# Layer 2 of a squared-relu network by seven half-size products in place of eight, behind relative-bias attention

## Chip, cores and metric

One core of a Trainium2 chip (trn2). The metric is the device time of one execution in microseconds, of the slowest core (here the only one). Executions of one kernel differ by 0.2 to 1.3%. A part of the spread goes with the clock that TensorE was granted.

## The reference

Attention with a bias that depends on the distance of query and key (8 batches, 8 heads, 576 positions, 64 channels a head), whose output, as 4608 tokens of 512 channels, goes through two layers with a squared relu:

```python
scores = scale * q @ k.T + bias[bucket(|i - j|)]
x = softmax(scores) @ v                  # -> [4608, 512]
h = maximum(x @ w_in, 0.0)               # w_in  [512, 2048]
out = (h * h) @ w_out                    # w_out [2048, 512], float32 out
```

## The kernel before

The program is written as a list of operations with assumed durations. A small scheduler (`Plan`) places them in time, each engine taking the earliest ready operation, and the instructions are emitted in that order. The order of every engine is therefore fixed ahead; at run time an engine only waits for the results it needs. Changing any duration or constant reorders all engines.

The tokens go through the two layers in nine groups of 512 (`GT`). Layer 1 of a group is 16 blocks of four matmuls; each is followed by a relu on ScalarE and a square on VectorE into `g`. Layer 2 of the group before runs between those blocks:

```python
# layer 2 of group g-1, before
tiles = [(m, 0, 512) for m in range(4)]
if g == NG:
    tiles[-1:] = [(3, 0, 256), (3, 256, 256)]     # the very last tile in halves
for m, c0, cn in tiles:
    bank = Buf(r_g)                                # one of 3 PSUM banks
    for part in range(4):
        def f2(...):
            for nt in range(4 * part, 4 * part + 4):
                nc.tensor.matmul(g_ps[bank.slot][:, 0:cn], gs[gb.slot][:, nt, ts(m, 128)],
                                 w_out_sb[:, nt, c0 : c0 + cn], start=(nt == 0), stop=(nt == 15))
        ...
    # then one eviction PSUM -> y (ScalarE or VectorE, scaled) and a store
```

Attention of later batches runs in between as well. Its product with v uses one PSUM bank (`pv`) for both of its parts, so the second part waits until VectorE has taken the reciprocal and normalised the first (`x`). The PSUM tiles are two double banks for scores, one for `pv`, three for everything of the layers.

q and k are staged by whole batches (`NSTG` = 2), turned on TensorE for the first three batches (`DT_QK` = 3) and by transposing DMA after that.

The softmax here doesn't subtract the row's maximum and nothing guards it: scores larger than these inputs give would overflow.

## Time and profile before

| | before |
|---|---|
| time, median (all runs) | 388.05 us (387.28 to 388.28) |
| span in the profile | 385.6 us |
| TensorE, ScalarE, VectorE, GpSimd busy | 96%, 68%, 51%, 41% |
| layer 2: matmuls, spacing | 560 of 512 columns at 216 ns and 32 of 256 at 109 ns |
| TensorE idle from 40 us to the last group (369 us) | 0.2 us |

TensorE's busy share is modelled, and matmuls overlap in it (a 512-column one is listed with 380 ns but the next starts 216 ns later). So the spacing from start to start is what counts. The prediction below shows the lines and how to read them.

### The profile page before, as it was taken

How to read it: one execution, taken by the hardware profiler on the slowest of the kernel's cores; microseconds unless marked ns; L12 is line 12 of the kernel's file. 1: busy time of each engine (PE TensorE's matmuls, PEld its weight loads, DVE VectorE, ACT ScalarE, POOL GpSimd, SP SyncE). 2: the span in 40 equal slices, each digit the busy share in tenths (PEclk: the TensorE clock that was granted, in tenths of full speed). 3: DMA queues.
4: the chain of work that ended last, by engine and by line, in shares of the span. 5: the costliest groups of instructions: out<-in, count | busy, mean ns of one | idle time of the engine just before them, and what ended most of it. 6: DMA issues, size and time to landing. Idle time of an engine off the chain costs nothing.

```text
span 385.6 us, 8906 instructions
## 1 busy us (share of the span) xinstructions
PE 369.8 (96%) x3544; PEld 201.1 (52%) x3544; DVE 194.9 (51%) x494; ACT 263.9 (68%) x378; POOL 157.2 (41%) x286
## 2 busy tenths in 40 slices
PE   2879999999999999999999999999999999999996
PEld 2557455664545455554557855454544555444444
DVE  5889563965635555564526653555356452422200
ACT  2898985888856886787767876957478653634421
POOL 7984710679446544747454455535420000000000
PEclk9999999999999999999999999999999999999999
DMA  7999994499988999969989699889940122001012
GB/s 102 147 201 175 176 191 55 53 108 93 131 113 133 98 119 108 139 79 143 112 136 88 85 102 159 88 92 114 137 115 27 36 73 73 0 27 54 31 54 83
DMA packets 144202, 39.04 MB, mean 101 GB/s; under 512 B 130592, under 2 KB 139680, under 8 KB 144160
## 3 DMA queue, kind: packets, MB, share of 16 engines
q0 software_dynamic: 94432, 18.36, 60.8%
q1 hardware_dynamic: 49488, 19.98, 24.7%
q8 instruction: 28, 0.46, 0.5%
q10 hardware_dynamic: 240, 0.13, 0.2%
q14 instruction: 14, 0.11, 0.1%
HBM read 36.87 MB, written 9.44 MB: 120 GB/s over the span
## 4 chain that ended last, share of the span: by engine, by line
PE 90%; DVE 3%; DMA 3%; ACT 2%; issue 1%; SPq 1%; POOL 0%; DVEq 0%; ACTq 0%
PE f L914 33%; PE f L864 31%; PE pv L759 9%; PE st L622 8%; PE pv L752 3%; PE st L671 2%; PE st L646 2%; DMA kt<-ks 1%; DMA far_sb<-in_bias_table_dram 1%; PE f L577 1%; ACT pt L633 1%; DVE pt L714 1%; DVE qt L541 1%; PE f L326 1%; DVE x L781 0%
## 5 line engine op out<-in xcount | busy, mean ns | idle before, releaser
L633 ACT ACTIVATE pt<-st 128x1024 f16<-128x1024 f32 x128 | 126.5, 1023 | 35.1 <-PE st L622 35.0
L864 PE MATMUL f<-w_out_sb,g 128*128 128x512 f16 (+1 forms) x592 | 141.2, 374 | 0.0
L914 PE MATMUL f<-xt,w_in_sb 128*128 128x512 f16 (+1 forms) x640 | 140.1, 358 | 0.2 <-ACT xt L539 0.2
L935 ACT ACTIVATE rt<-f 128x512 f16<-128x512 f32 x144 | 85.5, 599 | 41.6 <-PE f L914 40.4
L945 DVE TENSOR_TENSOR g<-rt 128x512 f16<-128x512 f16 x144 | 60.6, 421 | 67.9 <-ACT rt L935 67.0
L914 PEld LDWEIGHTS <-w_in_sb 128*128 128x128 f16 x640 | 59.5, 98 | 61.5 <-issue 9.6
L864 PEld LDWEIGHTS <-g 128*128 128x128 f16 x592 | 54.3, 98 | 59.6 <-issue 8.1
L714 DVE TENSOR_TENSOR pt<-pt,tb_sb 128x512 f16<-128x512 f16 (+2 forms) x96 | 58.9, 624 | 35.8 <-ACT pt L633 35.7
L759 PE MATMUL pv<-va,pt 128*128 128x65 f16 x1280 | 54.6, 193 | 0.0
L759 PEld LDWEIGHTS <-pt 128*128 128x128 f16 x1280 | 50.2, 97 | 4.6 <-issue 0.3
L604 POOL COPY qz<-qt 64x64 f16<-64x64 f16 x55 | 16.3, 297 | 78.1 <-DMA qt<-qs 46.9
L255 POOL DMA_DIRECT2D qs<-in_q_dram x57 | 40.7, 731 | 4.9 <-PE f L914 3.4
L622 PE MATMUL st<-qt,kt 64*128 64x512 f16 x256 | 40.2, 386 | 2.6 <-ACT pt L633 1.2
L255 POOL DMA_DIRECT2D ks<-in_k_dram x57 | 40.8, 749 | 1.4 <-DMA ks<-in_k_dram 1.0
L752 PE MATMUL pv<-vm,pm 128*128 128x130 f16 x160 | 35.4, 221 | 0.3 <-DVE x L781 0.3
L884 ACT ACTIVATE y<-f 128x512 f32<-128x512 f32 (+1 forms) x25 | 14.5, 580 | 26.1 <-PE f L864 25.8
L781 DVE TENSOR_TENSOR x<-pv,r 128x384 f16<-128x384 f32 x64 | 31.3, 489 | 1.7
L604 POOL COPY kz<-kt 64x64 f16<-64x64 f16 x53 | 14.8, 278 | 41.4 <-DMA kt<-ks 36.1
L776 DVE RECIPROCAL r<-pv 128x6 f32<-128x6 f32 x64 | 12.0, 187 | 37.7 <-PE pv L759 37.7
L255 POOL DMA_DIRECT2D va<-in_v_dram x36 | 30.8, 877 | 0.3
L681 ACT ACTIVATE pm<-st 128x576 f16<-128x576 f32 x32 | 20.8, 651 | 3.7 <-PE st L671 3.6
L656 ACT ACTIVATE pt<-st 128x512 f16<-128x512 f32 x32 | 19.2, 599 | 5.2 <-PE st L646 5.1
(49 smaller groups left out, 164.5 us busy)
## 6 DMA issues: line engine op xcount, KB each, us to landing
out_dram<-y SPq DMA_DIRECT2D x35, 256.0 KB, 2.3
va<-in_v_dram POOLq DMA_DIRECT2D x28, 128.0 KB, 6.2
qs<-in_q_dram POOLq DMA_DIRECT2D x40, 64.0 KB, 3.1
ks<-in_k_dram POOLq DMA_DIRECT2D x40, 64.0 KB, 3.1
w_in_sb<-in_moe_w_in_dram POOLq DMA_DIRECT2D x4, 512.0 KB, 7.2
w_out_sb<-in_moe_w_out_dram POOLq DMA_DIRECT2D x4, 512.0 KB, 9.1
xt<-x SPq DMA_TRANSPOSE x48, 3.0
qs<-in_q_dram POOLq DMA_DIRECT2D x4, 144.0 KB, 5.0
```

What stands on the lines that cost most here:

```text
L255: lambda: io(eng.dma_start(out=out_(), in_=in_())),
L604: io(eng.tensor_copy(out=dst[qb.slot][rw, rw], in_=src[qb.slot][rw, 512:576]))
L622: nc.tensor.matmul(sets_ps[st.slot][:, e, :], kt[rw, ts(jt, 128)], qt[rw, 0:512], start=True, stop=True,)
L633: nc.scalar.activation(out=p5(pts[pb.slot])[:, jt, :, 0:512], in_=sets_ps[st.slot], func=EXPF, scale=SCALE)
L714: io(nc.vector.tensor_tensor(out=a, in0=a, in1=t, op=MULT))
L752: nc.tensor.matmul(ps[:, i, :, :], pm[:, c : c + 128], vm[:, hp, :, 0:65], start=True, stop=False)
L759: nc.tensor.matmul(ps[:, i, e, :], pt[:, (2 * jt + e) * S + c : (2 * jt + e) * S + c + 128], va[:, jt, 2 * hp + e, 0:65], start=False, sto ...
L781: nc.vector.tensor_tensor(out=xs[xb.slot][:, hp, qt0 : qt0 + nq, :].rearrange("p t (e d) -> p t e d", e=2), in0=ps[:, :, :, 0:64], in1=rs[ ...
L864: nc.tensor.matmul(g_ps[bank.slot][:, 0:cn], gs[gb.slot][:, nt, ts(m, 128)], w_out_sb[:, nt, c0 : c0 + cn], start=(nt == 0), stop=(nt == 15),)
L914: nc.tensor.matmul(g_ps[bank.slot][:, a:z], w_in_sb[:, kk, ts(nt, 128)], xt_sb[:, kk, c : c + z - a], start=(kk == 0), stop=(kk == 3),)
L935: io(nc.scalar.activation(out=rts[rb.slot], in_=g_ps[bank.slot], func=RELUF))
L945: nc.vector.tensor_tensor(out=gs[gb1.slot][:, nt, :], in0=rts[rb.slot], in1=rts[rb.slot], op=MULT)
```

## The change

Split the 512 tokens of a group and the 2048 inner and 512 output channels of layer 2 in two each. The ordinary product then needs eight products of quarter matrices; Strassen's scheme (in Winograd's form) needs seven, at the price of sums: four of weights (once), four of activations (each group) and additions when the products are evicted. VectorE had half its time free, TensorE none, so work is moved from the one to the other.

Activations are the quarters `a11 a12 / a21 a22`. With S1 = a21 - a22, S2 = a11 - S1, S3 = a21 - a11, S4 = a12 - S2 (signs folded into the weight sums T), the products are taken in the order 1, 2, 6, 5, 3, 7, 4, in the last group 1, 6, 2, 5, 7, 3, 4. Products 2, 3 and 4 accumulate in the banks of 1, 5 and 7, and each of those must be read in between, since its value is needed alone too.

```diff
+        prod = {   # bank, left, right, sums of activations it needs
+            1: ("a", a11, w11, []),  2: ("a", a12, w21, []),  3: ("c", S4, w22, [4]),
+            4: ("d", a22, T4, []),   5: ("c", S1, T1, [1]),   6: ("b", S2, T2, [2]),  7: ("d", S3, T3, [3]) }
+        for i in P_ORDER:
+            for s_ in range(2):                      # two halves of 128 tokens
+                for c in range(8):
+                    nc.tensor.matmul(g_ps[bank[bk].slot][:, ts(s_, 256)], left(c, s_), right(c), ...)
+            # eviction: y = psum * OSC, or y = psum * OSC + other y (scalar_tensor_tensor on VectorE)
+    def sums_of_activations(g):                      # VectorE, 8 instructions of 128 x 1024 fp16 a group
+        for c0 in (0, 4):
+            for to in (3, 1, 2, 4):
+                nc.vector.tensor_tensor(out=out_, in0=a, in1=b_, op=subtract)
```

(The new lines are abridged; the table stands for the views that the code builds.) The sums need 24 KB a partition, of which some 17 KB are won by staging q and k and keeping x by pairs of heads instead of batches (`NSTG` 2 to 5, `NX` 2 to 5 with smaller buffers) and a ring of three batches for xt (`XB` 4 to 3). The fourth batch is now turned on TensorE too (`DT_QK` 3 to 4), up to three groups may give relus to VectorE (`RELU_DVE` 0 to 3), the order of the first loads (`ORDER`) and two small rings (`NRT` 4 to 3, `NY` 3 to 4) are different, and the pace constants of the scheduler are retuned:

```diff
-DT_QK = 3
-PERIOD, LEAD, FAST, FASTN = 8500.0, 11600.0, 4500, 8
-AHEAD, G0, GP = 7200.0, 42600.0, 36700.0
+DT_QK = 4
+PERIOD, LEAD, FAST, FASTN = 9800.0, 7200.0, 5100.0, 8
+AHEAD, G0, GP = 8700.0, 28800.0, 41600.0
```

More of the change, by code (lines that the diff above doesn't have):

```diff
@@ L27 @@
 NG = B * S // GT
-XB = 4
+XB = 3
 XR = XB * S
-DT_QK = 3
-PERIOD, LEAD, FAST, FASTN = 8500.0, 11600.0, 4500, 8
-AHEAD, G0, GP = 7200.0, 42600.0, 36700.0
+DT_QK = 4
+PERIOD, LEAD, FAST, FASTN = 9800.0, 7200.0, 5100.0, 8
+AHEAD, G0, GP = 8700.0, 28800.0, 41600.0
 DT_X = 2
-RELU_DVE = 0
-NSTG, NQK, NPT, NV, NX, NGB, NRT, NY = 2, 4, 2, 3, 2, 2, 4, 3
-SIX = 3
-ORDER = "i0 i1 q0 q1 k1 k0 i2 o0 v i3 o1 o2 o3"
+RELU_DVE = 3
+NSTG, NQK, NPT, NV, NX, NGB, NRT, NY = 5, 4, 2, 3, 5, 2, 3, 4
+P_ORDER = "1 2 6 5 3 7 4"
+P_LAST = "1 6 2 5 7 3 4"
+SIX = 4
+ORDER = "q0 i0 q1 i1 k0 v k1 i2 o0 o1 i3 o2 o3"
+HALF = GT // 2
 def _bucket(n):
@@ L221 @@
     oh_sb = sb("oh_sb", [128, 512])
-    stg = [[sb(f"{n}s{i}", [128, 6 * 512]) for n in "qk"] for i in range(NSTG)]
+    stg = [[sb(f"{n}s{i}", [128, 12 * D]) for n in "qk"] for i in range(NSTG)]
     qts = [sb(f"qt{i}", [128, 640]) for i in range(NQK)]
@@ L231 @@
     v4s = [sb(f"vm{i}", [128, 4, 2, VW]) for i in range(NV)]
-    xs = [sb(f"x{i}", [128, 4, 5, 128]) for i in range(NX)]
+    xs = [sb(f"x{i}", [128, 5, 128]) for i in range(NX)]
     xt_sb = sb("xt", [128, 4, XR + 64])
+    wt_sb = sb("wt", [128, 3, 8, 256])
+    ss = [sb(f"s{i}", [128, 8, 2, 128]) for i in (2, 3, 4)]
     gs = [sb(f"g{i}", [128, 16, GT]) for i in range(NGB)]
@@ L246 @@
     r_gb, r_rt, r_y, r_r = Ring(NGB), Ring(NRT), Ring(NY), Ring(2)
+    r_s = {i: Ring(1) for i in (2, 3, 4)}
     def loader(eng_name, eng, out_, in_, packets, deps=(), bufs=(), due=0.0):
@@ L368 @@
                 P.add(
-                    {"DVE": 320.0},
-                    lambda i=i, w=w: io(nc.vector.memset(stg[i][w][96:128, 0:2560].rearrange("p (c t d) -> p c t d", c=4, t=5)[:, :, 4, :].bitcast(FP32), 0.0)),
+                    {"DVE": 90.0},
+                    lambda i=i, w=w: io(nc.vector.memset(stg[i][w][96:128, 512:640].bitcast(FP32), 0.0)),
                     due=40 + i,
@@ L390 @@
             )
-    b_stg = [Buf(r_stg) for _ in range(B)]
+    b_stg = [Buf(r_stg) for _ in range(4 * B)]
     b_v = [Buf(r_v) for _ in range(B)]
@@ L405, in six @@
     def six(t):
-        return t[0:96, :].rearrange("p (h c) -> p h c", h=H)
+        return t[0:96, :].rearrange("p (h c) -> p h c", h=2)
     def rows(t):
-        return t[:, 0:2560].rearrange("p (c t d) -> p c t d", c=4, t=5)
-    def load_six(b, w, h0, nh):
-        src = (q, k)[w]
-        l = load(
-            "POOL", nc.gpsimd,
-            lambda: six(stg[b_stg[b].slot][w])[:, h0 : h0 + nh, :],
-            const(src[b, h0 : h0 + nh].rearrange("h (p j) d -> p h (j d)", j=6)),
-            96 * nh * 75, (), [b_stg[b]], pdue(),
-        )
-        for hp in range(h0 // 2, (h0 + nh) // 2):
-            l_qk[b, w, hp] = [l]
@@ L422, in load_qk, with load_six @@
-    def load_qk(b, w):
-        src = (q, k)[w]
-        tails = [
+        return t[:, 0:640].rearrange("p (t d) -> p t d", t=5)
+    def load_six(p, w):
+        b, hp = divmod(p, 4)
+        src = (q, k)[w][b, 2 * hp : 2 * hp + 2]
+        l_qk[p, w] = [
             load(
                 "POOL", nc.gpsimd,
-                lambda e=e: rows(stg[b_stg[b].slot][w])[0:64, :, 4, ds(64 * e, D)],
-                const(src[b, e::2, 512:S, :].transpose([1, 0, 2])),
-                256 * 34.5, first, [b_stg[b]], pdue(),
+                lambda: six(stg[b_stg[p].slot][w]),
+                const(src.rearrange("h (p j) d -> p h (j d)", j=6)),
+                192 * 75, (), [b_stg[p]], pdue(),
+            )
+        ]
@@ L430, in load_qk, with load_rows @@
+    def load_rows(p, w):
+        b, hp = divmod(p, 4)
+        src = (q, k)[w][b, 2 * hp : 2 * hp + 2]
+        l_qk[p, w] = [
+            load(
+                "POOL", nc.gpsimd,
+                lambda e=e: rows(stg[b_stg[p].slot][w])[:, 0:4, ds(64 * e, D)],
+                const(src[e, 0:512, :].rearrange("(t p) d -> p t d", p=128)),
+                512 * 34.5, first, [b_stg[p]], pdue(),
             )
             for e in range(2)
-        ]
-        for hp in range(4):
-            l_qk[b, w, hp] = tails + [
-                load(
-                    "POOL", nc.gpsimd,
-                    lambda hp=hp, e=e: rows(stg[b_stg[b].slot][w])[:, hp, 0:4, ds(64 * e, D)],
-                    const(src[b, 2 * hp + e, 0:512, :].rearrange("(t p) d -> p t d", p=128)),
-                    512 * 34.5, first, [b_stg[b]], pdue(),
-                )
-                for e in range(2)
-            ]
+        ] + [
+            load(
+                "POOL", nc.gpsimd,
+                lambda: stg[b_stg[p].slot][w][0:64, 512:640].rearrange("p (e d) -> p e d", e=2),
+                const(src[:, 512:S, :].rearrange("e p d -> p e d")),
+                128 * 34.5, first, [b_stg[p]], pdue(),
+            )
+        ]
@@ L500 @@
         for w in range(2):
-            load_six(0, w, 2 * hp, 2)
+            load_six(hp, w)
         if hp == 1:
@@ L514 @@
         elif step[0] in "qk":
-            load_six(1, "qk".index(step[0]), 4 * int(step[1]), 4)
+            for p in range(4 + 2 * int(step[1]), 6 + 2 * int(step[1])):
+                load_six(p, "qk".index(step[0]))
         else:
@@ L518 @@
     for b in range(2, B):
-        for w in range(2):
-            if b < SIX:
-                load_six(b, w, 0, 8)
-            else:
-                load_qk(b, w)
+        for p in range(4 * b, 4 * b + 4):
+            for w in range(2):
+                (load_six if b < SIX else load_rows)(p, w)
         load_v(b)
@@ L560, in pair @@
                         nc.sync.dma_start_transpose(
-                            out=dst[qb.slot].rearrange("p (t d) -> p t d", d=128), in_=rows(stg[b_stg[b].slot][w])[:, hp].rearrange("p t d -> p (t d)")
+                            out=dst[qb.slot].rearrange("p (t d) -> p t d", d=128), in_=stg[b_stg[p].slot][w][:, 0:640]
                         )
                     ),
-                    l_qk[b, w, hp], [qb, b_stg[b]], T - 6000, after,
+                    l_qk[p, w], [qb, b_stg[p]], T - 6000, after,
                 )
-                evac.append(P.add({"DMA": 1160.0}, None, [o], [qb, b_stg[b]], -1e9))
+                evac.append(P.add({"DMA": 1160.0}, None, [o], [qb, b_stg[p]], -1e9))
                 continue
@@ L571, in tr @@
                 ps = g_ps[bank.slot].bitcast(FP16)
-                t = stg[b_stg[b].slot][w]
+                t = stg[b_stg[p].slot][w]
                 if b < SIX:
@@ L577, in tr @@
                                 nc.tensor.transpose(
-                                    ps[ds(64 * e, 64), ts(j, 96)], six(t)[:, 2 * hp + e, ts(j, D)],
+                                    ps[ds(64 * e, 64), ts(j, 96)], six(t)[:, e, ts(j, D)],
                                     id_sb[0:96, 0:96],
@@ L583, in tr @@
                     for j in range(5):
-                        io(nc.tensor.transpose(ps[:, ts(j, 128)], rows(t)[:, hp, j, :], id_sb))
-            o = P.add({"PE": 12 * 36.0 if b < SIX else 5 * mm(128)}, tr, l_qk[b, w, hp] + [l_id], [bank, b_stg[b]], T - 3000, after, "c" if b < SIX else "f")
+                        io(nc.tensor.transpose(ps[:, ts(j, 128)], rows(t)[:, j, :], id_sb))
+            o = P.add({"PE": 12 * 36.0 if b < SIX else 5 * mm(128)}, tr, l_qk[p, w] + [l_id], [bank, b_stg[p]], T - 3000, after, "c" if b < SIX else "f")
             def turned(bank=bank):
@@ L737, in pair @@
         ]
-        if hp == 0:
-            x_bufs[b] = Buf(r_x)
-        xb = x_bufs[b]
+        xb = x_bufs[p] = Buf(r_x)
         norms = []
@@ L781, in norm @@
                     nc.vector.tensor_tensor(
-                        out=xs[xb.slot][:, hp, qt0 : qt0 + nq, :].rearrange("p t (e d) -> p t e d", e=2),
+                        out=xs[xb.slot][:, qt0 : qt0 + nq, :].rearrange("p t (e d) -> p t e d", e=2),
                         in0=ps[:, :, :, 0:64],
@@ L797, in pair @@
                         nc.sync.dma_start_transpose(
-                            out=xt_sb[:, hp, c : c + 128 * nq].rearrange("p (t d) -> p t d", d=128), in_=xs[xb.slot][:, hp, qt0 : qt0 + nq, :].rearrange("p t d -> p (t d)")
+                            out=xt_sb[:, hp, c : c + 128 * nq].rearrange("p (t d) -> p t d", d=128), in_=xs[xb.slot][:, qt0 : qt0 + nq, :].rearrange("p t d -> p (t d)")
                         )
@@ L809, in x_turn @@
     def x_turn(b, norms):
-        xb = x_bufs[b]
+        xb = [x_bufs[4 * b + hp] for hp in range(4)]
         T = nominal(4 * b + 3)
@@ L818, in tr @@
                 for kk in range(4):
-                    io(nc.tensor.transpose(ps[:, ts(kk, 128)], xs[xb.slot][:, kk, qt, :], id_sb))
+                    io(nc.tensor.transpose(ps[:, ts(kk, 128)], xs[xb[kk].slot][:, qt, :], id_sb))
             deps = [n_[0 if qt < 3 else 1] for n_ in norms]
-            o = P.add({"PE": 4 * mm(128)}, tr, deps, [bank, xb], T, 0.0, "f")
+            o = P.add({"PE": 4 * mm(128)}, tr, deps, [bank] + xb, T, 0.0, "f")
             t0 = (b % XB) * S + qt * 128
@@ L846, with fourth, sums_of_weights @@
     f2s = {}
+    def fourth(gb, eo, t, c0, n):
+        g_ = gs[gb.slot].rearrange("p (c o) (s t m) -> p c o s t m", o=2, s=2, t=2)
+        return g_[:, c0 : c0 + n, eo, :, t, :]
+    w4 = w_out_sb.rearrange("p (c o) (h d) -> p c o h d", o=2, h=2)
+    def sums_of_weights():
+        done = []
+        for c0 in (0, 4):
+            cs = ds(c0, 4)
+            l = [l_wout[c0 // 2], l_wout[c0 // 2 + 1]]
+            t2, t3, t4 = (wt_sb[:, i, cs] for i in range(3))
+            w11, w12, w21, w22 = (w4[:, cs, o, h] for o in range(2) for h in range(2))
+            o = None
+            for out_, a, b_, op in (
+                (t3, w22, w12, mybir.AluOpType.add),
+                (w12, w12, w11, mybir.AluOpType.subtract),
+                (t2, w22, w12, mybir.AluOpType.add),
+                (t4, w21, t2, mybir.AluOpType.subtract),
+            ):
+                o = P.add(
+                    {"DVE": dve(1024, 2.0)},
+                    lambda out_=out_, a=a, b_=b_, op=op: io(nc.vector.tensor_tensor(out=out_, in0=a, in1=b_, op=op)),
+                    l + [o], (), 1e5,
+                )
+            done.append(o)
+        return done
@@ new lines, in sums_of_activations, with add @@
+    def sums_of_activations(g):
+        gb = g_bufs[g]
+        sb_ = s_bufs[g] = {i: Buf(r_s[i]) for i in (2, 3, 4)}
+        for c0 in (0, 4):
+            o = None
+            for to in (3, 1, 2, 4):
+                def add(to=to, c0=c0):
+                    a11, a12, a21, a22 = (fourth(gb, eo, t, c0, 4) for t in range(2) for eo in range(2))
+                    s = {i: ss[i - 2][:, c0 : c0 + 4] for i in (2, 3, 4)}
+                    out_, a, b_ = {
+                        3: (s[3], a21, a11), 1: (a21, a21, a22), 2: (s[2], a11, a21), 4: (s[4], a12, s[2])
+                    }[to]
+                    io(nc.vector.tensor_tensor(out=out_, in0=a, in1=b_, op=mybir.AluOpType.subtract))
+                o = P.add(
+                    {"DVE": dve(1024, 2.0)}, add, squares[g][2 * c0 : 2 * c0 + 8] + [o],
+                    [gb] + ([sb_[to]] if to > 1 else []) + ([sb_[2]] if to == 4 else []), G0 + GP * g - 5e4,
+                )
+                s_done.setdefault((g, to), []).append(o)
@@ new lines, in second, with mul, atom, fin @@
+    def second(g):
+        gb, sb_ = g_bufs[g], s_bufs[g]
+        bank = {i: Buf(r_g) for i in "abcd"}
+        y = {i: Buf(r_y) for i in ("u", "v", "11", "12")}
+        rows_ = out[ds(g * GT, GT), :].rearrange("(s t p) c -> t p s c", s=2, t=2)
+        prod = {
+            1: ("a", lambda c, s: fourth(gb, 0, 0, c, 1)[:, 0, s], lambda c: w4[:, c, 0, 0], []),
+            2: ("a", lambda c, s: fourth(gb, 1, 0, c, 1)[:, 0, s], lambda c: w4[:, c, 1, 0], []),
+            3: ("c", lambda c, s: ss[2][:, c, s], lambda c: w4[:, c, 1, 1], [4]),
+            4: ("d", lambda c, s: fourth(gb, 1, 1, c, 1)[:, 0, s], lambda c: wt_sb[:, 2, c], []),
+            5: ("c", lambda c, s: fourth(gb, 0, 1, c, 1)[:, 0, s], lambda c: w4[:, c, 0, 1], [1]),
+            6: ("b", lambda c, s: ss[0][:, c, s], lambda c: wt_sb[:, 0, c], [2]),
+            7: ("d", lambda c, s: ss[1][:, c, s], lambda c: wt_sb[:, 1, c], [3]),
+        }
+        reads = {
+            1: [("u", None, None)], 6: [("u", "u", None)], 2: [("11", None, (0, 0))], 5: [("v", "u", None)],
+            7: [("v", "v", (1, 1))], 3: [("12", "u", (0, 1))], 4: [("u", "u", (1, 0))],
+        }
+        lastly = {1: [], 6: [1], 2: [1], 5: [], 7: [], 3: [5], 4: [7]}
+        read_of, u_users = {}, []
+        atoms = []
+        for i in (int(x) for x in (P_LAST if g == NG - 1 else P_ORDER).split()):
+            bk, left, right, ns = prod[i]
+            for s_ in range(2):
+                def mul(i=i, s_=s_, bk=bk, left=left, right=right):
+                    for c in range(8):
+                        io(
+                            nc.tensor.matmul(
+                                g_ps[bank[bk].slot][:, ts(s_, HALF)], left(c, s_), right(c),
+                                start=(c == 0 and s_ == 0 and i in (1, 6, 5, 7)), stop=(c == 7),
+                                skip_group_check=True,
+                            )
+                        )
+                def atom(d, i=i, s_=s_, bk=bk, ns=ns, mul=mul):
+                    deps = d + [x for n in ns for x in s_done[g, n]] + [read_of[x] for x in lastly[i] if bk != "b"]
+                    deps += squares[g] if not ns else []
+                    deps += l_wout if i in (1, 2) else t_done
+                    return P.add(
+                        {"PE": 8 * mm(HALF)}, mul, deps,
+                        [bank[bk], gb] + [sb_[n] for n in ns if n > 1], 1e6, 0.0, "f",
+                    )
+                atoms.append(atom)
+            def fin(o, i=i, bk=bk):
+                (to, plus, where), = reads[i]
+                def ev():
+                    dst, ps = ys[y[to].slot], g_ps[bank[bk].slot]
+                    if plus is not None:
+                        io(
+                            nc.vector.scalar_tensor_tensor(
+                                out=dst, in0=ps, scalar=OSC, in1=ys[y[plus].slot], op0=MULT, op1=mybir.AluOpType.add
+                            )
+                        )
+                    elif e.eng == "ACT":
+                        io(nc.scalar.activation(out=dst, in_=ps, func=COPYF, scale=OSC))
+                    else:
+                        io(nc.vector.tensor_scalar_mul(out=dst, in0=ps, scalar1=OSC))
+                deps = [o]
+                if plus == "u":
+                    deps.append(read_of[1 if i == 6 else 6])
+                if plus == "v":
+                    deps.append(read_of[5])
+                if i == 4:
+                    deps += [read_of[3], read_of[5]]
+                bufs = [bank[bk], y[to]] + ([y[plus]] if plus not in (None, to) else [])
+                engs = {"DVE": dve(512)} if plus is not None else {"DVE": dve(512), "ACT": act(512)}
+                e = read_of[i] = P.add(engs, ev, deps, bufs, 0.0)
+                if where is not None:
+                    t, h = where
+                    P.add(
+                        {"SP": 700.0},
+                        lambda: io(
+                            nc.sync.dma_start(
+                                out=rows_[t][:, :, ts(h, HALF)],
+                                in_=ys[y[to].slot].rearrange("p (s d) -> p s d", s=2),
+                            )
+                        ),
+                        [e], [y[to]], 0.0,
+                    )
+            atoms.append(fin)
+        return atoms
@@ L848, in layers @@
     def layers(g):
         due = G0 + GP * g
-        atoms2 = []
-        if g >= 1:
-            gb = g_bufs[g - 1]
-            tiles = [(m, 0, 512) for m in range(4)]
-            if g == NG:
-                tiles[-1:] = [(3, 0, 256), (3, 256, 256)]
-            for m, c0, cn in tiles:
-                bank = Buf(r_g)
-                for part in range(4):
-                    def f2(m=m, part=part, bank=bank, gb=gb, c0=c0, cn=cn):
-                        for nt in range(4 * part, 4 * part + 4):
-                            io(
-                                nc.tensor.matmul(
-                                    g_ps[bank.slot][:, 0:cn], gs[gb.slot][:, nt, ts(m, 128)],
-                                    w_out_sb[:, nt, c0 : c0 + cn], start=(nt == 0), stop=(nt == 15),
-                                )
-                            )
-                    atoms2.append(
-                        lambda d, f2=f2, bank=bank, gb=gb, part=part, cn=cn: P.add(
-                            {"PE": 4 * mm(cn)}, f2, d + squares[g - 1][4 * part : 4 * part + 4] + [l_wout[part]],
-                            [bank, gb], 1e6, 0.0, "f",
-                        )
-                    )
-                    if part == 3:
-                        def fin(o, bank=bank, row=(g - 1) * GT + m * 128, c0=c0, cn=cn):
-                            yb = Buf(r_y)
-                            def ev():
-                                y, ps = ys[yb.slot][:, 0:cn], g_ps[bank.slot][:, 0:cn]
-                                if e.eng == "ACT":
-                                    io(nc.scalar.activation(out=y, in_=ps, func=COPYF, scale=OSC))
-                                else:
-                                    io(nc.vector.tensor_scalar_mul(out=y, in0=ps, scalar1=OSC))
-                            e = P.add({"DVE": dve(cn), "ACT": act(cn)}, ev, [o], [bank, yb], 0.0)
-                            P.add(
-                                {"SP": 700.0},
-                                lambda: io(
-                                    nc.sync.dma_start(
-                                        out=out[ds(row, 128), c0 : c0 + cn], in_=ys[yb.slot][:, 0:cn]
-                                    )
-                                ),
-                                [e], [yb], 0.0,
-                            )
-                        atoms2.append(fin)
@@ L900, in layers @@
+        atoms2 = second(g - 1) if g >= 1 else []
         atoms1 = []
@@ L923, in layers @@
         last = None
-        for i in range(24):
+        for i in range(16):
             if i < len(atoms1):
@@ L959, in layers @@
                     i2 += 1
-    squares, g_bufs = {}, {}
+        if g < NG:
+            sums_of_activations(g)
+    squares, g_bufs, s_bufs, s_done = {}, {}, {}, {}
+    t_done = sums_of_weights()
     g = 0
```

## The prediction

> **What bounds the kernel now.** I read the page first, part 1 (busy time), part 2 (slices) and part 4 (the chain that ended last), to see which engine sets the end and from when on.
>
> ```profile
> PE 369.8 (96%) x3544; PEld 201.1 (52%) x3544; DVE 194.9 (51%) x494; ACT 263.9 (68%) x378; POOL 157.2 (41%) x286
> ...
> PE   2879999999999999999999999999999999999996
> ...
> PEclk9999999999999999999999999999999999999999
> ...
> PE 90%; DVE 3%; DMA 3%; ACT 2%; issue 1%; SPq 1%; POOL 0%; DVEq 0%; ACTq 0%
> PE f L914 33%; PE f L864 31%; PE pv L759 9%; PE st L622 8%; PE pv L752 3%; PE st L671 2%; PE st L646 2%; DMA kt<-ks 1%; DMA far_sb<-in_bias_table_dram 1%; PE f L577 1%; ACT pt L633 1%; DVE pt L714 1%; DVE qt L541 1%; PE f L326 1%; DVE x L78
> ```
>
> TensorE is full from slice 4 on at full clock and makes up 90% of the chain. Layer 1 (L914) and layer 2 (L864) are a third of it each. VectorE has half its time free.
>
> A busy PE is only a modelled figure, so I looked at the chain in order of time, where each piece runs from one start to the next, and at the stage table:
>
> ```profile
> 203.45 0.86 PE f L864 x4
> 204.31 0.87 PE f L914 x8
> ...
> 369.74 12.51 PE L864 MATMUL f<-w_out_sb,g 128*128 128x512 f16 x73
> ...
> 40.00:320.00 280.00, 279.82 (x2670) 151.18 (x2669) 149.88 (x360) 208.63 (x295) 126.90 (x230) 1.00 0.97 106
> ```
>
> The first two lines are the most useful of the whole profile. Four matmuls of 512 columns take 0.86 us, so 216 ns each. Eight matmuls of 256 columns (layer 1, in a group that wraps round the ring of xt; form 128x256 in the groups) take 0.87 us, 109 ns each, with a fresh 128x128 weight load for every one. Half-size matmuls therefore cost half: the weight load stays hidden. The stage table says that from 40 to 320 us PE idles 0.2 us in 280. Nothing is waiting there; only less PE work can shorten it.
>
> For the cost of what VectorE gets, the groups by form:
>
> ```profile
> L945 DVE TENSOR_TENSOR g<-rt 128x512 f16<-128x512 f16 x144 | 60.6, 421 | 67.9 <-ACT rt L935 67.0
> L714 DVE TENSOR_TENSOR pt<-pt,tb_sb 128x1536 f16<-128x1536 f16 x32 | 30.6, 956 | 21.4 <-ACT pt L633 21.4
> L884 ACT ACTIVATE y<-f 128x512 f32<-128x512 f32 x23 | 13.7, 597 | 23.5 <-PE f L864 23.3
> L886 DVE TENSOR_SCALAR y<-f 128x512 f32<-128x512 f32 x12 | 8.3, 691 | 9.0 <-PE f L864 9.0
> ```
>
> 512 fp16 elements take 421 ns and 1536 take 956, so 0.52 ns an element and some 154 ns fixed; 1024 take about 690 ns. An eviction of 512 fp32 from PSUM on VectorE takes 691 ns.
>
> **What the Trainium skill says.** "TensorE: Matmul & The Clock Gate", section Back-to-back issue gap, gives N/2.4 + 2.5 ns for a warm matmul: 216 ns at 512 columns and 109 at 256. The trace agrees to the nanosecond. The same section calls that an isolated figure and puts sustained N=512 at 131 ns; the trace contradicts it, with 216 ns sustained over hundreds of matmuls. "VectorE: DVE Perf Modes", section The perf-mode tier table, has tensor_tensor at double rate for 16-bit data in SBUF and at single rate with any PSUM operand; the 0.52 ns an element above and the 691 ns eviction agree. "PSUM — Partial Sum Buffer", section PSUM bank collisions raise a hardware error, says that two engines must not touch one bank and quadrant at the same time. That is why the new code lets a product that accumulates onto an earlier one in the same bank wait until that one has been read. No run shows a collision. "SBUF — State Buffer", section Who interferes with whom: a DVE instruction with two SBUF inputs contends with GpSimd instructions that read SBUF. The new sums are such, so the small qz and kz copies on POOL (297 and 278 ns) may stretch; the present trace does not separate that.
>
> **The change part by part.**
>
> Layer 2, removed: 9 groups x 64 matmuls of 512 columns = 576 x 216 ns = 124.4 us. Added: 9 x 7 products x 2 row halves x 8 = 1008 matmuls of 256 columns x 109 ns = 109.9 us. Net **-14.5 us**, all on the path, since PE has no gaps there.
>
> Transposes: q and k of a fourth batch are turned on PE in place of by DMA (DT_QK 3 to 4): 4 pairs x 2 turns of twelve small matmuls. One turn takes 0.28 us next to another, 0.35 to 0.40 us with its change of mode (the chain has x24 in 0.70 us and x12 in 0.40): 8 x 0.36 = **+2.9 us**. XB 4 to 3 only moves the wraps of xt to other groups, and splits cost nothing measurable (8 halves = 4 wholes).
>
> VectorE: activation sums 9 x 8 x 0.69 = 49.7 us; weight sums 8 x 0.69 = 5.5; evictions with an addition 9 x 5 x about 0.69 = 31; perhaps half of the 18 plain evictions, 6, against 8.3 of today; evictions of the extra turns some 5; relus that the first three groups may give it some 10. Together 194.9 becomes about **295 us**, or 78% of the span. ScalarE falls by some 15 us. Neither is the bound by its sum: a group period of about 40 us holds 6.7 us of squares, 5.5 of sums, 4.5 of evictions and, at 4.2 pairs x 3.5 us, 15 of attention, 32 in all. So nearly all of this lies beside PE; it costs only where PE waits for a particular result.
>
> Waits that I see in the code. Each group has three places where a product accumulates into a bank that must be read in between (2 after 1, 3 after 5, 4 after 7): about 0.7 us of eviction and 0.3 of handover, against one interleaved layer-1 block (0.86 us). Product 1 needs all sixteen squares, where today's first block needs four. While there is layer-1 or attention work in between this is filled, but PE's order is fixed ahead, so misjudged durations turn into gaps. I put **+2 us** for all of them (estimate: some 0.2 us a group).
>
> The end: the last group has nothing to fill with. After the last layer-1 block come a relu (0.60) and a square (0.42) with handovers, about 1.2 us, before product 1 starts; then product 6 needs S2, three sums after the last square (2.1 us), against 1.74 us of product 1: 0.4 more. Now the last eviction is 256 columns on ScalarE (0.38 us) and 128 KB out (1.9 us to landing); then 512 columns with an addition (0.7) and 256 KB (2.3). Together 1.2 + 0.4 + 0.7 = **+2.3 us**.
>
> The start: PE's first 40 us have some 12 us idle, fed by transfers and by ScalarE. Loading by pairs lets pieces arrive in finer grain, relus may go to VectorE in the first groups, and the order is retuned. But the first layer-1 matmul came at 39.3 us behind a fixed chain, and the first 5 us are the first load. I give it **-2 us**.
>
> Sum: -14.5 + 2.9 + 2 + 2.3 - 2 = -9.3, so 388.08 - 9.3 = **378.8 us**.
>
> **The rivals.** First, *VectorE becomes a second bound*: with 78% load and a strict order, relu-square-sum-product chains and mid-bank reads make PE wait 1 to 1.5 us in every group. For it: three PSUM banks serve layer 1 and layer 2, and each extra read holds one about 1 us longer; S2, S3 and S4 have one buffer each, so a group's sums cannot start before the previous group's products 6, 7 and 3 are done. Against: the sums are needed only after products 1 and 2, some 7 us later with the layer-1 blocks between them. It would make 384 to 390 us and eat the gain. Second, *nothing is lost*: the new order hides every wait and the start gains 4 us; 388.08 - 14.5 + 2.9 + 2.3 - 4 = 374.8 us. Third, *loads become the wait*: staging shrinks from two batches to five pairs, so a load waits for a turn five pairs back and holds the queue behind it, as POOL issues in order. Against: five pairs at 8 to 10 us is over 40 us of lead, while a load lands in 3 to 5 us; POOL is busy 41%. For it: in the first 40 us the transfers are at 90% and more. It would cost 2 to 5 us early: 381 to 384 us.
>
> **Range and chances.** The 14.5 us is nearly certain, so slower by 2% would need over 20 us of new waits. "Faster by over 2%" means under 380.3 us, only 1.5 us above my figure, while my uncertainty on waits and start is about 3 us either way; the schedule's constants have all been retuned, which speaks for few gaps. 8 in 10: 374.5 to 384.5 us. Faster 0.62, within 2% 0.36, slower 0.02.
>
> **What would show it right or wrong.** Layer 2 as about 1008 matmuls at 109 ns from start to start (eight in 0.87 us), PE's idle time between 40 us and the last group under 3 us, VectorE near 295 us with sums near 690 ns each, and a gap of 1 to 2 us before the last group's product 1. Wrong: half-size matmuls above 115 ns, waits of PE for y or for the sums that add up to more than 5 us, or a first layer-1 matmul later than 41 us.

## The result

The changed kernel takes 379.19 us (378.98 to 379.79, 4 runs) against 388.05 (387.28 to 388.28): ratio 0.9777, 95% interval 0.976 to 0.9795, so faster by over 2%, and 0.4 us from the predicted 378.8. A later set of runs gave 379.07 us and 0.9771. Ratios here are the mean time of one kernel's runs over that of the other's of the same rounds, so they are not quite the ratio of the quoted medians.

The page of the changed kernel: engine totals, TensorE's and VectorE's slices, and the chain that ended last, by engine and by line (L1012 is layer 1, L934 layer 2).

```profile
PE 360.3 (96%) x4120; PEld 246.2 (65%) x4120; DVE 270.3 (72%) x628; ACT 256.6 (68%) x366; POOL 170.1 (45%) x298
...
PE   2879999999999999999999999999999999999985
...
DVE  4799798999779657966597569756865593583652
...
PE 87%; DVE 6%; ACT 3%; DMA 2%; issue 1%; POOL 0%; ACTq 0%; DVEq 0%; POOLq 0%
PE f L1012 34%; PE f L934 28%; PE pv L763 9%; PE st L628 8%; PE pv L756 2%; ACT pt L639 2%; PE st L677 2%; PE st L652 2%; DMA ks<-in_k_dram 2%; PE f L583 1%; DVE pt L720 1%; DVE s L896 1%; PE f L332 1%; DVE x L785 1%; ACT pt L662 0%
```

TensorE is as full as before and its busy time is 9.5 us less; VectorE has gone from 51% to 72%. Layer 2's share of the chain has fallen from 31% to 28%.

The chain in order of time in the middle of the changed kernel (start, length, what), for the spacing of the half-size products:

```profile
121.33 0.87 PE f L934 x8
...
124.85 0.87 PE f L934 x8
```

Eight take 0.87 us, 109 ns each, as predicted from layer 1's half-size matmuls. So layer 2 is 1008 x 109 = 109.9 us, against 560 x 216 + 32 x 109 = 124.4 before.

What VectorE got (groups; busy us, mean ns, idle before):

```profile
L896 DVE TENSOR_TENSOR s<-g 128x1024 f16<-128x1024 f16 x36 | 24.8, 688 | 0.2
L896 DVE TENSOR_TENSOR s<-g,s 128x1024 f16<-128x1024 f16 x18 | 12.4, 690 | 0.4
L896 DVE TENSOR_TENSOR g<-g 128x1024 f16<-128x1024 f16 x18 | 12.4, 689 | 0.4
...
L959 DVE SCALAR_TENSOR_TENSOR y<-f,y 128x512 f32<-128x512 f32 x45 | 31.0, 689 | 14.7 <-PE f L934 14.2
```

49.6 us of activation sums and 31.0 us of adding evictions, both of the predicted size. Did TensorE wait for them? The stages of the changed kernel (length; busy time and count of PE, weight loads, DVE, ACT, POOL; clock; DMA):

```profile
40.00:361.00 321.00, 320.66 (x3483) 216.94 (x3482) 234.15 (x513) 225.64 (x323) 135.67 (x238) 1.00 0.84 97
```

In 321 us TensorE is idle for 0.34 us. (A matmul is listed as busy until some 0.16 us after the next one could start, so shorter delays do not show here; the section on the prediction adds them up.) The one wait of some size comes after that, in the last group. This is the timeline there (start, length, engine, line; in brackets the idle time and what ended it):

```profile
359.43 1.91 PE L934 MATMUL f<-w_out_sb,g 128*128 128x256 f16 x16
...
361.18 0.60 PE L934 MATMUL f<-wt,s 128*128 128x256 f16 x4
...
362.05 0.69 DVE L896 TENSOR_TENSOR s<-g 128x1024 f16<-128x1024 f16 x1
...
362.80 1.48 PE L934 MATMUL f<-wt,s 128*128 128x256 f16 x12 [1.02 <-DVE s L896]
```

Product 1 follows layer 1's last block without a gap (its first matmuls read only squares that are long done), four matmuls of product 6 run on the first half of S2, and then TensorE waits 1.02 us until VectorE has made the second half.

### The profile page after: what moved, and what is told of

It is laid out like the page before. It is cut to its first block, busy times and chain, and to the rows that moved or that the text cites. A ratio compares the mean times of both kernels' runs of the same rounds, so it can differ in the third digit from the quotient of the medians.

```text
span 377.1 us, 10222 instructions
## 1 busy us (share of the span) xinstructions
PE 360.3 (96%) x4120; PEld 246.2 (65%) x4120; DVE 270.3 (72%) x628; ACT 256.6 (68%) x366; POOL 170.1 (45%) x298
## 4 chain that ended last, share of the span: by engine, by line
PE 87%; DVE 6%; ACT 3%; DMA 2%; issue 1%; POOL 0%; ACTq 0%; DVEq 0%; POOLq 0%
PE f L1012 34%; PE f L934 28%; PE pv L763 9%; PE st L628 8%; PE pv L756 2%; ACT pt L639 2%; PE st L677 2%; PE st L652 2%; DMA ks<-in_k_dram 2%; PE f L583 1%; DVE pt L720 1%; DVE s L896 1%; PE f L332 1%; DVE x L785 1%; ACT pt L662 0%
## 5 line engine op out<-in xcount | busy, mean ns | idle before, releaser
L1012 PE MATMUL f<-xt,w_in_sb 128*128 128x512 f16 (+4 forms) x704 | 143.0, 341 | 0.1
L1033 ACT ACTIVATE rt<-f 128x512 f16<-128x512 f32 x136 | 81.3, 598 | 64.8 <-PE f L1012 62.6
L1012 PEld LDWEIGHTS <-w_in_sb 128*128 128x128 f16 x704 | 62.8, 98 | 49.0 <-issue 8.2
L934 PEld LDWEIGHTS <-g 128*128 128x128 f16 x576 | 54.3, 98 | 14.5 <-issue 5.1
L934 PE MATMUL f<-w_out_sb,g 128*128 128x256 f16 x432 | 54.3, 273 | 0.0
L934 PEld LDWEIGHTS <-s 128*128 128x128 f16 x432 | 40.6, 98 | 12.7 <-issue 3.8
L261 POOL DMA_DIRECT2D qs<-in_q_dram x64 | 44.7, 712 | 4.7 <-PE f L583 3.2
L261 POOL DMA_DIRECT2D ks<-in_k_dram x64 | 44.4, 707 | 2.9 <-DMA w_out_sb<-in_moe_w_out_dram 1.8
L959 DVE SCALAR_TENSOR_TENSOR y<-f,y 128x512 f32<-128x512 f32 x45 | 31.0, 689 | 14.7 <-PE f L934 14.2
L934 PE MATMUL f<-wt,s 128*128 128x256 f16 x288 | 37.1, 273 | 1.0 <-DVE s L896 1.0
L610 POOL COPY kz<-kt 64x64 f16<-64x64 f16 x51 | 18.1, 356 | 29.8 <-DMA kt<-ks 18.0
L896 DVE TENSOR_TENSOR s<-g 128x1024 f16<-128x1024 f16 x36 | 24.8, 688 | 0.2
```

Source lines behind the costliest of these rows:

```text
L261: lambda: io(eng.dma_start(out=out_(), in_=in_())),
L610: io(eng.tensor_copy(out=dst[qb.slot][rw, rw], in_=src[qb.slot][rw, 512:576]))
L934: nc.tensor.matmul(g_ps[bank[bk].slot][:, ts(s_, HALF)], left(c, s_), right(c), start=(c == 0 and s_ == 0 and i in (1, 6, 5, 7)), stop=(c ...
L1012: nc.tensor.matmul(g_ps[bank.slot][:, a:z], w_in_sb[:, kk, ts(nt, 128)], xt_sb[:, kk, c : c + z - a], start=(kk == 0), stop=(kk == 3),)
L1033: io(nc.scalar.activation(out=rts[rb.slot], in_=g_ps[bank.slot], func=RELUF))
```

## The experiments

In all of them the kernel before ran beside it on the same chip; it took 388.0 to 388.6 us (medians). Four edits leave TensorE's order of instructions exactly as it is in the changed kernel (`sums_untold`, `sums_third`, `sums_once`, `squares_again`), and two leave all but the last group's sums on VectorE (`tail_fine`, `tail_s2`); this was checked on the emitted order.

### Eight products again, the rest of the change kept

```diff
-        atoms2 = second(g - 1) if g >= 1 else []
+        atoms2 = <the tiles of the kernel before>      # and no sums of weights or activations
```

> The changed kernel with layer 2 put back to eight products (64 matmuls of 512 columns a group, no sums), all else of the change kept: staging and x by pairs, ring of three, fourth batch turned on TensorE, new schedule constants. Theory (TensorE's column count sets the time): 379.2 + 14.5 for the columns - 1.2 for the wait of the last group's product on S2, which goes, - 0.7 for the shorter last eviction and store = 391.8 us, so slower than the kernel before by about 1% (the 2.8 us of extra turns). Rival (the staging by pairs and the new order brought part of the gain): 388 us or less. Rival (the seven products hide further waits of their own): clearly under 391.

Measured: 391.33 us (390.91 to 391.58), ratio to before 1.0079. The companion changes cost 391.33 - 388.55 = 2.8 us by themselves, and the seven products gain 391.33 - 379.19 = 12.1 us (379.07 later: 12.3). That is the 14.5 us of columns less 2.4 us, of which 1.0 us is the wait for S2 and about 0.8 us the later end. Taken together, the staging, the turns and the new order are no hidden gain. This does not say what each of them does: with the seven products, the pace constants alone turn out below to be worth 3.6 us.

### The fourth batch turned by DMA again

```diff
-DT_QK = 4
-SIX = 4
+DT_QK = 3
+SIX = 3
```

> The changed kernel with the fourth batch's q and k loaded by rows and turned by DMA again, as before the change. Theory: eight turns fewer on TensorE at some 0.34 us each, so 379.2 - 2.7 = 376.5 us. Rival (that batch was moved to TensorE because its transfers come too late while the weights and q, k, v are still loading): TensorE waits for qt or kt between 50 and 110 us and the time is 379 us or more.

Measured: 383.84 us (382.25 to 386.1), ratio 0.9894: slower than the changed kernel by 4.6 us (by 3 us in the one execution at a mean clock of 1.00, the 382.25), so my expectation fell. The rival's size came true but not its place. What TensorE waited for (who waited for whom: us in total, times, longest):

```profile
PE f L934 <- ACT y L964: 2.5, 4, 0.7
PE f L1012 <- DMA xt<-x: 2.2, 3, 1.5
```

None of this is before 150 us, and none is on qt or kt. The first line is product 2 waiting for the reading of product 1 out of the shared bank, with nothing in between: the reordered plan put the sixteen matmuls of one product directly ahead of the next. In the changed kernel there is other work there. The second line is layer 1 waiting for the transposing DMA of x. Why the plan came out so with these constants I did not settle; the saved turns are real (from start to start they take 9.3 us of TensorE in place of 11.9), but the order lost more than they gave.

### The pace constants of the kernel before

```diff
-PERIOD, LEAD, FAST, FASTN = 9800.0, 7200.0, 5100.0, 8
-AHEAD, G0, GP = 8700.0, 28800.0, 41600.0
-RELU_DVE = 3
+PERIOD, LEAD, FAST, FASTN = 8500.0, 11600.0, 4500, 8
+AHEAD, G0, GP = 7200.0, 42600.0, 36700.0
+RELU_DVE = 0
```

> The changed kernel with the pace constants of the kernel before (period, lead, fast, ahead, start and period of the groups, no relu on VectorE). Theory (TensorE has enough ready work under either order): 379 to 382 us. Rival (the retuned order is what keeps the seven products free of waits): 384 us or more, with idle TensorE in the middle of the span.

Measured: 382.76 us (382.17 to 383.49), ratio 0.9863. The stages of this run (columns as above):

```profile
40.00:80.00 40.00, 37.59 (x484) 21.89 (x482) 34.75 (x81) 36.31 (x54) 22.32 (x40) 1.00 1.05 138
80.00:120.00 40.00, 39.64 (x516) 26.47 (x510) 29.93 (x72) 31.09 (x43) 25.08 (x42) 1.00 1.16 110
120.00:360.00 240.00, 240.00 (x2461) 165.96 (x2458) 163.37 (x355) 159.57 (x230) 86.10 (x155) 1.00 0.80 87
```

It lies a little above the theory's band and under the rival's. Of the loss of 3.6 us, some 2.4 us is idle time of TensorE between 40 and 120 us (2.8 us here, 0.34 in the changed kernel). Most of it lies before 80 us, where ScalarE is busy 36 of 40 us; after 120 us TensorE is full. The rest was not located. So the retuned constants, `RELU_DVE` among them, are worth about two fifths of the whole gain, and work early. About half of these waits (1.4 us) are for ScalarE and the others for VectorE: that the constants work by relieving ScalarE is likely, but not shown.

### The sums done twice, in the same order

```diff
-                    io(nc.vector.tensor_tensor(out=out_, in0=a, in1=b_, op=...subtract))
+                    for _ in range(1 if to == 1 else 2):
+                        io(nc.vector.tensor_tensor(out=out_, in0=a, in1=b_, op=...subtract))
```

> Every activation sum that is not in place is done twice, without the schedule knowing it, so every engine's order stays the same; 54 more VectorE instructions of 0.69 us, 37 us more, VectorE busy about 307 us (82%). Theory (VectorE lies beside TensorE): only the last group shows it, where S2 comes 1.4 us later, and perhaps 1 us in all other places: 380.6 to 381.6 us. Rival (VectorE is close to being a second bound): 386 us or more, with waits of TensorE on sums or on y in most groups. The POOL copies qz and kz, 344 and 356 ns now against 297 and 278 before the change, should get longer again if the VectorE sums hold them up.

Measured: 402.86 us (400.43 to 405.74), ratio 1.0382. The theory failed clearly: 34 us more busy time on VectorE (304.1 against 270.3) cost 23.7 us. (In the one execution at a mean clock of 1.00, 400.43 us, it cost 21 us; the slowest, 405.74 us, had a clock of 0.981.) Yet VectorE is busy only 76% of the span. The waits of TensorE, and one of them in the timeline:

```profile
PE pv L756 <- DVE x L785: 7.7, 7, 2.1
PE f L583 <- DMA qs<-in_q_dram: 5.2, 1, 5.2
PE f L1013 <- DVE y L960: 3.0, 4, 1.1
PE pv L763 <- DVE pt L720: 2.5, 2, 1.8
PE f L935 <- DVE y L967: 2.3, 1, 2.3
PE f L935 <- DVE s L897: 2.3, 1, 2.3
```

```profile
209.74 1.41 DVE L897 TENSOR_TENSOR s<-g 128x1024 f16<-128x1024 f16 x2
...
211.18 1.42 DVE L897 TENSOR_TENSOR s<-g,s 128x1024 f16<-128x1024 f16 x2
212.52 0.68 DVE L967 TENSOR_SCALAR y<-f 128x512 f32<-128x512 f32 x1
...
213.25 1.03 PE L935 MATMUL f<-w_out_sb,g 128*128 128x256 f16 x8 [2.33 <-DVE y L967]
```

Only the last of the six waits is for a sum. (The second is the first load, which every version has.) The others are for `x`, `y` and `pt`: results that TensorE needs to reuse a PSUM bank or to begin a product with v. In the longest of these waits a row of sums goes by on VectorE first (1.3 of 2.1 us, 1.4 of 1.8 us, 1.6 of 2.3 us); in several of the short ones no sum runs. In the timeline, product 2 may not touch bank a until product 1 has been read; that reading takes 0.68 us but first four sums go by.

### The same with the schedule told of it

The edit is as above, with the planned duration doubled too.

> The doubled sums again, now with their cost known to the schedule, which orders all engines anew. Theory: as with the unknown doubling, about 381 us, since TensorE's work is the same. Rival (VectorE at 82% cannot be hidden by any order): 386 us or more.

Measured: 396.62 us (395.12 to 399.28), ratio 1.0227. My theory of some 381 us fell. Reordering wins back 6 of 24 us. So it was not only that the fixed order was wrong; within this plan the extra load does not fit. Of what is left, 3.7 us are a single wait for S2 in the last group.

### The same load in single short pieces

```diff
-  io(tensor_tensor(out=gs[..][:, nt, :], in0=rts[..], in1=rts[..], op=MULT))
+  [io(tensor_tensor(out=gs[..][:, nt, :], in0=rts[..], in1=rts[..], op=MULT)) for _ in range(2 if nt < 10 else 1)]
```

> Ten of every sixteen squares are done twice, unknown to the schedule: 90 instructions of 0.42 us, 38 us more on VectorE, as much as the doubled sums added, but in single short pieces in place of bursts of eight to fourteen. Theory now: it is the length of the burst that stands in VectorE's line ahead of the normalisation of x and of the evictions, not the total, that holds TensorE up; so well under the 22 us of the doubled sums: 381 to 388 us. Rival (VectorE's total load is near its bound): some 400 us as with the doubled sums.

Measured: 385.13 us (383.93 to 386.33), ratio 0.9923. VectorE's busy time is 304.3 us, the same as with the doubled sums to 0.2 us, but the cost is 6.0 us in place of 23.7. From 40 us to the last group, first here and then with the doubled sums:

```profile
40.00:366.00 326.00, 320.21 (x3468) 215.81 (x3465) 266.71 (x600) 225.16 (x322) 135.21 (x237) 1.00 0.82 95
```

```profile
40.00:378.00 338.00, 321.98 (x3465) 216.63 (x3464) 261.99 (x557) 224.86 (x321) 134.94 (x238) 0.99 0.78 91
```

With squares VectorE is at 82% and TensorE idles 5.8 us; with sums at 78% and idles 16.0. So the total load alone does not decide. What differs is where the work stands: a square more delays what is behind it by 0.42 us, a doubled row of sums by 2 to 4 us (three to six more sums of 0.69 us). The two edits also sit at different places in a group, so length and place are not fully separated.

### Only S3 twice

```diff
+                    for _ in range(2 if to == 3 else 1):
```

> Only the S3 sums are done twice, unknown to the schedule: 18 instructions, 12.4 us more on VectorE. Doubling all three sums added 37 us and cost 22. If the cost is in proportion: 379.2 + 7.5 = 386.7 us. If there is slack that absorbs the first part: 380 to 382 us.

Measured: 381.46 us (381.13 to 381.77), ratio 0.9826: 2.4 us for 12.4 us of work. So the first third of the extra work costs 0.2 us per us, all of it 0.6. There is slack, and it ends soon. Of the 2.4 us, 0.7 are in the last group (a wait for S2 of 1.7 us in place of 1.0).

### Without the sums (wrong result)

```diff
+                    if g == 0:
                         io(nc.vector.tensor_tensor(out=out_, in0=a, in1=b_, op=...subtract))
```

> Wrong result on purpose: the activation sums are computed for the first group only, all orders else unchanged; VectorE falls by 64 x 0.69 = 44 us to about 226. It asks whether the sums cost anything in the changed kernel beyond the 1.2 us wait of the last group. Theory: 379.2 - 1.2 - at most 0.5 = 377.5 to 378 us. Rival (they hold TensorE up in many small places): 375 us or less.

Measured: 377.48 us (377.36 to 378.99), ratio 0.9738; result wrong. That is 1.6 to 1.7 us under the changed kernel. Taking 39 us off VectorE (270.3 to 231.3) gives that much and no more, and 1.0 of it is the wait of the last group, which is gone. Beside that wait, the 49.6 us of sums cost next to nothing in the changed kernel.

### The last group's sums, finer

```diff
-        for c0 in (0, 4):
+        cuts = (0, 4, 8) if g < NG - 1 else (0, 4, 6, 7, 8)
+        for c0, c1 in zip(cuts, cuts[1:]):
```

> The changed kernel, with the second half of the last group's sums cut into pieces of two, one and one (12 smaller VectorE instructions in place of four of 1024). TensorE's order is unchanged, VectorE's up to the last group too. Theory: the 1.2 us for which the last group's product 6 waits for S2 falls to about 0.1, so 1.1 us off: 378.1 us against 379.2. Rival (the wait only moves on to product 5's or 7's operand or to an eviction): 379 us.

Measured: 380.28 us (379.76 to 381.36), ratio 0.9799 (0.9772 to 0.9825): no gain. The wait was split and grew, from 1.02 to 1.75 us:

```profile
363.69 0.28 PE L936 MATMUL f<-wt,s 128*128 128x256 f16 x1 [0.85 <-DVE s L898]
...
364.87 1.16 PE L936 MATMUL f<-wt,s 128*128 128x256 f16 x9 [0.90 <-DVE s L898]
```

Each cut still made S4, which nobody needed yet, before the next cut's S2, and the twelve short instructions took 4.0 us on VectorE against 2.8 us for the four long ones.

### The last group's sums in the order in which they are needed

```diff
+        else:   # last group
+            steps = [(c0, c1, to) for c0, c1 in ((0, 4), (4, 7), (7, 8)) for to in (3, 1, 2)]
+            steps += [(0, 4, 4), (4, 8, 4)]
```

> The changed kernel with the last group's sums reordered: S3, S1, S2 first over parts of four, three and one, both halves of S4 last; TensorE's order unchanged. The cut of tail_fine only moved the wait, because the S4 pieces and four short chains stood in line before the last S2. Theory: here the last S2 comes about 1 us sooner than in the changed kernel, and 0.8 to 1.1 us come off: 378.2 us. Rival (some other operand or eviction is next in line): no gain.

Measured: 378.11 us (377.74 to 379.95, 6 runs), ratio 0.9751 (0.9726 to 0.9777), beside the changed kernel's 379.07 us and 0.9771 (0.9746 to 0.9796):

> The changed kernel itself, unaltered, as the yardstick for the runs of this call on the same chip: 379 to 380 us, ratio to the kernel before 0.978.

The chain of the new version in order of time shows the last group in one piece, where the changed kernel's chain goes through sums from 360.69 to 362.80:

```profile
357.88 1.73 PE f L1016 x8
359.61 12.37 PE f L938 x112
```

```profile
360.69 0.61 DVE s L896
...
362.05 0.70 DVE s L896
...
362.80 10.23 PE f L934 x92
```

112 matmuls in 12.37 us is 110 ns each: the wait is gone. The medians differ by 0.96 us, as much as the trace shows; the two intervals overlap, so by the times alone it would not be proven. Sorted afterwards by mean clock, the executions at 0.998 and above do separate: four of the new version at 377.74 to 378.32 us, five of the changed kernel at 378.53 to 379.11 us. It is the fastest version with a correct result.

## Why the prediction was right, step by step

To check the terms, every matmul of the traces of both kernels was counted from its start to the start of the next one, without the listed idle time.

- **TensorE's columns set the time.** Right, and the largest term: -14.5 us predicted, 124.4 to 109.9 us by count and spacing. The reason it could be had before building is that the kernel before already ran half-size matmuls in layer 1. From start to start, layer 2 falls from 126.6 to 111.8 us, but layer 1 rises from 126.2 to 127.8 us, so the two together give 13.3 us. The prediction put layer 1's change at nothing. In part the loss only moved over from layer 2: a matmul of layer 1 right before a product of scores is followed some 0.1 us late, and there are 30 of these in place of 16.
- **Extra turns, +2.9 us.** Right: from start to start they take 11.9 us in place of 9.2, so 2.7 us more. (That all companion changes together cost 2.8 us in `eight` does not show this, since the pace constants among them may gain, as they do in `old_pace`.) That taking the turns back would gain was not in the prediction but in the expectation of `dt3`, and was wrong.
- **Waits, +2 us.** Too much: 0.34 us idle from 40 us to the last group. The two waits that I named, bank and squares, are filled by layer 1 and attention. Nor does product 1 need all sixteen squares: it reads eight of them. What is lost instead lies in pieces too short for the waits: layer 1, as above, and the products of scores, which take 53.0 us in place of 51.7.
- **The end, +2.3 us.** In sum nearly right (1.0 us of waiting, and from the start of the last eviction to the end 4.1 us in place of 3.3, 1.8 together), but not as split: product 1 did not wait 1.2 us for the squares, since it starts with those long done, and S2 was 1.0 us late, not 0.4.
- **The start, -2 us.** Wrong in size: layer 1 begins at 38.95 us in place of 39.29, and TensorE's idle time in the first 40 us falls from 12.2 to 11.4 us, a gain of 0.8 us.
- **The sum, -9.3 us.** That it came so near is partly luck. With the waits, the end, the turns and the start as measured it would have been -10.7 us, and the spans of the two profiled executions differ by 8.5. The 2 us put down for waits stood in for losses of about that size, 1.2 us in the layers and 1.3 us in the scores, that the prediction did not have.
- **VectorE at 295 us.** Too high; 270.3. Only 8 relus went to it, not 15, only 5 plain evictions, and the extra turns gave it no more copies than before (16). The rest is overlap: neighbours on VectorE start up to 0.09 us before the one in front ends, and busy time counts that once. The durations add up to 293.5 us, 23.2 more than the busy time; before the change it was 206.1 and 11.2 more.
- **The rival "VectorE becomes a second bound"** did not come, but it was nearer than I gave it. I argued from busy time; `sums_untold` and `squares_again` show that this is not enough, and the waits point to the row of sums that stands ahead of an eviction. A quarter more of sums (S3 twice) costs 2.4 us, three quarters more (all but S1 twice) 24. The rival "loads become the wait" does not show after the first loads. There TensorE waits 2.1 us for the first k, where before it waited 2.0 us for `eb_sb`, a piece of the bias table.
- **Two reasons given beside the skill.** The banks must be read in between because a value would be lost when the next product is added to it; this would be so without any collision. And the eviction of 691 ns is a TENSOR_SCALAR, so it says nothing of tensor_tensor. The product that makes `x` is one with a PSUM operand: 384 elements take 557 ns and 256 take 424 in the changed kernel, 1.04 ns an element, twice the 0.52 that the prediction works out for fp16 in SBUF.

## What to carry to other kernels

When one engine is full from end to end, moving its work to another that is half idle can pay at most of the rate (here 12.1 of 14.5 us), and the spacing from start to start of instructions that already run in the wanted size tells the gain in advance. Judge the engine that takes the work not by its busy share alone but also by the longest row of instructions that can stand ahead of a result the full engine needs; the same 34 us cost 6 us in short single pieces and 24 us in rows. In such a plan, put what the next consumer needs first and leave the rest of a batch of sums for later.

## What the Trainium skill lacked or had wrong

- "TensorE: Matmul & The Clock Gate", section Back-to-back issue gap: the sustained 131 ns for N=512 is wrong for this kernel, which shows 216 ns over hundreds of matmuls with a weight load each; the formula N/2.4 + 2.5, called isolated there, holds at 512 (216 ns) and at 256 (109 ns).
- "TensorE: Matmul & The Clock Gate", section HAM oscillation — how this bites in real kernels: its rule of no idle gaps over some 3.4 us does not tell here when the clock falls. In `sums_twice` a wait of 3.68 us was followed by a clock of 0.56:

```profile
378.97 2.34 PE L935 MATMUL f<-wt,s 128*128 128x256 f16 x12 [3.68 <-DVE s L897]
...
379.00:382.70 3.70, 3.70 (x20) 2.73 (x21) 2.02 (x3) 0.00 (x0) 0.00 (x0) 0.56 0.02 4
```

But in `sums_untold` a wait of 2.06 us was followed by half clock (first line), and one of 2.33 us by full clock (second line):

```profile
69.10:72.50 3.40, 3.40 (x41) 2.82 (x41) 3.30 (x10) 1.10 (x2) 0.87 (x2) 0.50 0.77 95
...
213.30:217.00 3.70, 3.70 (x57) 2.66 (x57) 2.39 (x8) 1.30 (x2) 3.48 (x8) 1.00 1.55 99
```

And one execution of the changed kernel (`after_again`) had half clock from 23.7 to 27.1 us after waits of at most 0.57 us in the 3.7 us before, while the other profiled one, with the same waits at that place, kept 1.00. So the length of the gap alone does not decide:

```profile
23.70:27.10 3.40, 3.40 (x45) 2.41 (x44) 3.24 (x9) 2.36 (x4) 3.07 (x8) 0.50 1.27 204
```

- "SBUF — State Buffer", section Who interferes with whom, which has a VectorE instruction with two SBUF inputs contend with GpSimd's reads: the qz and kz copies on GpSimd went from 297 and 278 ns to 344 and 356 ns with the sums, but doubling the sums did not lengthen them further (344 and 336), and with eight products and no sums they already took 305 and 337, with the sums left out after the first group 350 and 298. The runs do not show the contention as a cause.
- No page says how to judge an engine's room for more work when it is strictly in order: 304 us busy on VectorE gave 402.9 us in one arrangement and 385.1 us in another.
